# Who asks for the transfer of the negated maxima in a windowed attention and SwiGLU kernel

## The chip, the core and the metric

The kernel runs on one core of a Trainium2 chip. The metric is the device time of one execution in microseconds (us), lower is better. The kernel before was run three times; the table below has the times, and the profile is of one more execution.

## The reference

`x` is 2048 tokens of 512 values in fp32. With `xn` the layer norm of `x`, two branches are computed and combined:

```python
xn = _layernorm(x, axis=-1)
s = _A_ref(xn, A_wqkv, A_wo)              # attention
g = _silu(_B_ref(xn, gate, up, down))     # (silu(xn @ gate) * (xn @ up)) @ down
return x + s * g
```

The attention has 32 heads of 16 values. A query sees the 256 keys up to its own (`0 <= q - k < 256`), the scores are scaled by 1/4 and go through a softmax, the outputs of the heads go through `wo`. The hidden width of the SwiGLU branch is 1792.

## The kernel before, in words

**Tiling.** The tokens are cut into four chunks of 512 (`TC`), the heads into eight groups of four (`NG`). A unit `u` is one group in one chunk, `c, g = divmod(u, 8)`, so there are 32 units. The dense work (projections `a`, values `vp`, gate `g` and up `u`, down `d`, output `s`) is done in fp32 accuracy by splitting each operand in a high and a low part (`wh`, `wl`, `xh`, `xl`, `hh`) and adding three products; all of these matmuls stand in one helper at line 463. TensorE works in two halves of 64 rows, each with its own list of matmuls, and the two lists run beside each other.

**A unit of attention.** In the order in which it happens:

1. `load_qk` (line 917) loads queries and keys of the unit from DRAM into `qs[u % 3]` and `ks[u % 3]`. Queries and keys fill 48 of the 64 rows of each half, and a 49th row of the keys holds ones.
2. `max_pair` (line 946) multiplies queries by keys (`b`, line 960), and VectorE takes the masked maximum of each row into a column of `m` (line 968). There are 16 such maxima steps in a unit.
3. `max_turn` (line 988) transposes `m` with two matmuls on TensorE into the bank `mt` (line 994), the first and second half of the rows; between them stands a one-column copy on VectorE (`ho`, line 460).
4. `neg` (line 1007) runs on ScalarE and writes the negated maxima to `ms` in SBUF (line 1009).
5. `put` (line 1015) moves `ms`, 8 KB, into rows 48 and 112 of `qs[u % 3]`. So the 49th row of the queries, times the 49th row of ones in the keys, subtracts the maximum within the matmul.
6. `prob_pair` (line 1063) multiplies keys by queries with 49 rows (`c`, line 1111). ScalarE takes the exponential (`p`, line 1072), GpSimd masks it (lines 1085 and 1089).
7. `pv_visit` (line 1128) multiplies `p` by the values (`pv`, line 1148). ScalarE and VectorE add the two halves (`ev`, lines 1164 and 1169), and the result goes to DRAM, to be divided and used by `Wo`.

**What sets the order.** Nothing is reordered after the program is written. A planner in the program itself walks a virtual clock and writes out the instructions of all engines in the order of its own plan. It keeps a queue for VectorE (`V`), ScalarE (`S`), GpSimd (`G`) and for DMA issues (`D`, all on SyncE's queue); `do` (line 107) adds an operation with the time from which it can run, a cost, and a slack that sets its priority. When an operation is planned, what follows is told that it ends at the engine's free time plus a latency (`LAT`: 0.17 us for ScalarE, line 105). `dma` (line 115) is `do` for the queue `D`: an issue costs 0.5 us, must wait until the oldest of the last eight transfers (`lanes`) is planned to have landed, and its own landing is planned as

```python
stream_at[0] = max(stream_at[0], t) + kb / 230.0
done = stream_at[0] + LAND          # LAND = 3.5
```

The dense units have a fixed order, made ahead of time (`dense_order`, line 1217). Attention work comes in three streams with due times in units of dense progress (`plan_attention`, line 1195): the maxima from `u + 0.02`, the transposes at `u + 0.8`, the first `c` at `u + 1.07`, `pv` at `u + 1.89`. In the main loop (line 1386) a piece of attention work goes ahead of dense work when it is due and its inputs are planned to be ready. For `c` that is `prob_ready` (line 1055): the transfer of the maxima has landed by plan (`ms_at`), two banks are free, and there is room for `p`.

**Queues.** All transfers go through `move` (line 90), by default on SyncE's queue. Only two of the first four tiles of `x` are asked for by ScalarE, in its own queue. The engines wait for each other through semaphores in the order written.

Of the kernel before, what the change touches and what calls it, by code (L numbers as in the profile page):

```python
# [55 lines left out]
def tile_window_attention_swiglu_gate(  # L56
# [10 lines left out]
    nc = tc.nc  # L67
# [16 lines left out]
    def sb(name, shape, dtype, kind, n):  # L84
        return pers.tile(shape, dtype, name=name, tag=ring(kind, n), bufs=1)

    def f32(ap):
        return ap.bitcast(F32)

    def move(dst, src, eng=nc.sync):  # L90
        if dst.dtype == F32R:
            dst = f32(dst)
        if src.dtype == F32R:
            src = f32(src)
        eng.dma_start(dst, src)  # L95
# [11 lines left out]
    def do(e, ready, cost, fn, then=None, slack=0.5, can=None, lat=None):  # L107
        seq[0] += 1
        queue[e].append((ready + slack, seq[0], ready, cost, fn, then, can, LAT.get(e, 0.0) if lat is None else lat))
# [5 lines left out]
    def dma(ready, fn, then=None, slack=0.5, kb=256, can=None, e="D"):  # L115
        def begun_at(t):
            stream_at[0] = max(stream_at[0], t) + kb / 230.0
            done = stream_at[0] + LAND
            lanes.append(done)
            lanes.pop(0)  # L120
            if then:
                then(done)

        do(e, ready, 0.5, fn, begun_at, slack, lambda: lanes[0] <= now[0] and (can is None or can()), 0.0)
# [52 lines left out]
    def bank(pool, name):  # L177
        tag = min((v, k) for k, v in pool.items() if v is not None)[1]
        pool[tag] = None
        return ps.tile([P, 512], F32, name=name, tag=tag, bufs=1), tag  # L180
# [5 lines left out]
    qs = [pers.tile([P, 2, TC], F32R, name=f"q{i}") for i in range(3)]  # L186
# [181 lines left out]
    def half(r):  # L368
        return slice(R * r, R * r + R)
# [89 lines left out]
    def handover(pb):  # L459
        nc.vector.tensor_copy(pers.tile([MW, 1], F32, name="ho", tag=ring("ho", 2), bufs=1), pb[:MW, 0:1])  # L460
# [454 lines left out]
    ms_at = {}  # L915
# [72 lines left out]
    def max_turn(u, r):  # L988
        if r == 0:
            mtp[u] = [*bank(rb_free, f"mt{u}"), None]  # L990
        pb, tag, _ = mtp[u]

        def go():
            nc.tensor.matmul(
                pb[:MW, R * r : R * r + R], mts[u % 2][half(r), :], ident[half(r), half(r)],
                is_transpose=True, start=True, stop=True,
            )

        if r == 0:
            def after(t):  # L1000
                mtp[u][2] = t

            extra[0].append((128, go, lambda t: do("V", t, 0.09, lambda: handover(pb), after, -1.0)))
            return
        box = []

        def neg():
            box.append(sb(f"ms{u}", [16, P], F32R, "ms", 2))
            nc.scalar.activation(box[0], pb[:16, :P], AF.Copy, scale=-1.0)

        def after_neg(t):
            rb_free[tag] = t
            dma(t, put, lambda t: ms_at.__setitem__(u, t), -3.0, 8)

        def put():
            move(qs[u % 3][48 : 113 : 64], box[0])

        extra[1].append((128, go, lambda t: do("S", t, 0.25, neg, after_neg, -1.0)))

# [173 lines left out]
    def plan_attention():  # L1195
        for u in range(NU):
            c = u // NG
            if u:
                marks.append((u - 1 + 0.3, load_qk, (u,)))
            for n in range(8):  # L1200
                streams[0].append((u + 0.02 + 0.1 * n, max_ready, max_pair, (u, n // 4, n % 4)))
            streams[0].append((u + 0.8, turn_ready, max_turn, (u, 0)))
            streams[0].append((u + 0.8, turn_ready, max_turn, (u, 1)))
            ne = 3 if c == 0 else 4
            for n in range(2 * ne):
                streams[1].append((u + 1.07 + 0.1 * n, prob_ready, prob_pair, (u, n // 2, n % 2)))
            streams[1].append((u + 1.89, pv_ready, pv_visit, (u, tuple(range(ne)))))
        for c in range(1, NCH):
            marks.append((8 * c - 4.9, load_x, (c,)))
            for k in range(KC):  # L1210
                streams[2].append((8 * c - 3.3 + 0.25 * k, xt_ready, xt_turn, (c, k)))
        for s in streams:
            s.reverse()
        marks.sort(key=lambda m: -m[0])
# [73 lines left out]
    extra = [[], []]  # L1288
# [97 lines left out]
    while True:  # L1386
# [11 lines left out]
        if not any(extra):  # L1398
            s = work[0] / PACE - LEAD
            for st in sorted(streams, key=lambda st: st[-1][0] if st else 1e9):  # L1400
# [7 lines left out]
                t = need(*a)  # L1408
# [20 lines left out]
        if os.environ.get("VIRT"):  # L1429
            u, i = stream[min(pos[0], len(stream) - 1)]  # L1430
# [40 lines left out]
```

## Time and profile before

| | |
|---|---|
| runs of the kernel before | 871.76 us median of 3 (870.12 to 876.5) |
| profiled execution, its own time | 871.37 us |
| its span, first to last instruction | 869.7 us |
| mean granted clock of TensorE | 0.999 |
| bytes moved by DMA, mean rate | 139.62 MB, 161 GB/s |

Lines of the profile name an engine, a line of the kernel, and the tile written and read (`q<-ms` is the transfer of this case). PE is TensorE's matmul, PEld its weight load, DVE VectorE, ACT ScalarE, POOL GpSimd, SP SyncE. A `q` behind an engine's name (SPq, ACTq) means its sequencer, which issues transfers. Times in a timeline are the start from the span's beginning and the length, both in us; a bracket gives the idle time of the engine before it and what ended that. A wait for several semaphores is put down to the one that came last. In lists of waits the numbers are the total, how often, and the longest.

### The profile page before, as it was taken

How to read it: one execution, taken by the hardware profiler on the slowest of the kernel's cores; microseconds unless marked ns; L12 is line 12 of the kernel's file. 1: busy time of each engine (PE TensorE's matmuls, PEld its weight loads, DVE VectorE, ACT ScalarE, POOL GpSimd, SP SyncE). 2: the span in 40 equal slices, each digit the busy share in tenths (PEclk: the TensorE clock that was granted, in tenths of full speed). 3: DMA queues.
4: the chain of work that ended last, by engine and by line, in shares of the span. 5: the costliest groups of instructions: out<-in, count | busy, mean ns of one | idle time of the engine just before them, and what ended most of it. 6: DMA issues, size and time to landing. Idle time of an engine off the chain costs nothing.

```text
span 869.7 us, 30126 instructions
## 1 busy us (share of the span) xinstructions
PE 859.5 (99%) x11966; PEld 798.1 (92%) x11966; DVE 499.1 (57%) x1650; ACT 489.9 (56%) x1046; POOL 627.4 (72%) x871
## 2 busy tenths in 40 slices
PE   9999999999999999999999999999999999999997
PEld 8899889899889998999999999899999999999897
DVE  5364466654765565766576666566555765554234
ACT  3345565555666466655566556655656665666431
POOL 5556587667777778767696798676768688869771
PEclk9999999999999999999999999999999999999999
DMA  5765846567676984766677987546666779644352
GB/s 148 187 167 121 221 115 168 126 162 167 148 198 180 251 201 105 152 156 133 155 184 194 214 200 181 129 145 151 158 150 173 174 187 209 162 130 112 108 126 74
DMA packets 69488, 139.62 MB, mean 161 GB/s; under 512 B 14546, under 2 KB 23250, under 8 KB 69348
## 3 DMA queue, kind: packets, MB, share of 16 engines
q1 hardware_dynamic: 69060, 137.18, 64.1%
q8 instruction: 94, 1.54, 0.8%
q10 hardware_dynamic: 288, 0.52, 0.2%
q14 instruction: 46, 0.38, 0.2%
HBM read 107.74 MB, written 29.62 MB: 158 GB/s over the span
## 4 chain that ended last, share of the span: by engine, by line
PE 93%; DMA 3%; DVE 1%; SPq 1%; POOL 0%; issue 0%; ACT 0%; ACTq 0%; DVEq 0%; POOLq 0%
PE u L463 18%; PE d L463 18%; PE g L463 17%; PE a L463 11%; PE pv L1148 8%; PE s L463 6%; PE c L1111 5%; PE vp L463 5%; PE b L960 4%; DMA q<-ms 1%; DMA r<-rd 1%; DMA xt<-x 1%; SPq L95 1%; DVE xt L291 0%; PE xp L481 0%
## 5 line engine op out<-in xcount | busy, mean ns | idle before, releaser
L434 POOL TENSOR_TENSOR wl<-wr,wh 128x512 fp32r<-128x512 f32 (+3 forms) x258 | 306.8, 1208 | 89.4 <-ACT wh L431 86.9
L968 DVE CUSTOM_DVE_ANT_0 jk<-b,maskb 128x384 bf16<-128x384 f32 (+2 forms) x512 | 271.5, 530 | 130.1 <-PE b L960 64.5
L1072 ACT ACTIVATE p<-c 128x384 f32<-128x384 f32 (+1 forms) x480 | 208.8, 489 | 127.1 <-PE c L1111 106.5
L463 PE MATMUL d<-wh,hh 64*128 64x256 f32 x1792 | 258.2, 278 | 0.0
L463 PEld LDWEIGHTS d<-wh,hh 64*128 64x128 f32 x1792 | 222.9, 185 | 1.0 <-issue 0.6
L463 PE MATMUL d<-wl,hh 64*128 64x256 f32 x896 | 201.3, 277 | 0.0
L431 ACT ACTIVATE wh<-wr 128x512 fp32r<-128x512 f32 (+3 forms) x258 | 142.2, 593 | 51.2 <-PE d L463 11.1
L463 PE MATMUL u<-xh,wh 64*128 64x512 f32 x448 | 167.3, 396 | 0.0
L463 PE MATMUL g<-xh,wh 64*128 64x512 f32 x448 | 167.2, 396 | 0.0
L463 PE MATMUL u<-xl,wh 64*128 64x512 f32 x448 | 166.9, 396 | 0.0
L463 PE MATMUL u<-xh,wl 64*128 64x512 f32 x448 | 166.9, 396 | 0.0
L463 PE MATMUL g<-xl,wh 64*128 64x512 f32 x448 | 166.5, 395 | 0.0
L463 PE MATMUL g<-xh,wl 64*128 64x512 f32 x448 | 164.8, 394 | 0.0
L1085 POOL TENSOR_SCALAR_AFFINE_SELECT p<-p 128x256 f32<-128x256 f32 x256 | 103.7, 410 | 77.1 <-ACT p L1072 75.6
L463 PEld LDWEIGHTS d<-wl,hh 64*128 64x128 f32 x896 | 144.4, 185 | 0.3
L960 PE MATMUL b<-k,q 48*128 48x384 f32 (+1 forms) x512 | 119.2, 333 | 0.0
L1111 PE MATMUL c<-q,k 49*128 49x384 f32 (+1 forms) x704 | 115.5, 302 | 2.3 <-DMA q<-ms 1.2
L1089 POOL TENSOR_SCALAR_AFFINE_SELECT p<-p 128x256 f32<-128x256 f32 x224 | 91.6, 410 | 13.2 <-ACT p L1072 13.1
L463 PE MATMUL a<-xh,wh 64*128 64x512 f32 x256 | 97.2, 394 | 0.0
L463 PE MATMUL a<-xh,wl 64*128 64x512 f32 x256 | 96.4, 392 | 0.0
L616 POOL TENSOR_TENSOR hh<-h,hh 128x512 fp32r<-128x512 f32 x56 | 72.5, 1295 | 33.0 <-ACT hh L612 32.7
L463 PE MATMUL a<-xl,wh 64*128 64x512 f32 x256 | 96.2, 393 | 0.0
(109 smaller groups left out, 2096.6 us busy)
## 6 DMA issues: line engine op xcount, KB each, us to landing
wr<-wgu SPq DMA_DIRECT2D x112, 256.0 KB
k<-qkd SPq DMA_DIRECT2D x48, 192.0 KB
wr<-wqk SPq DMA_DIRECT2D x32, 256.0 KB
qkd<-qkh SPq DMA_DIRECT2D x32, 256.0 KB
qkd<-qkl SPq DMA_DIRECT2D x32, 256.0 KB
q<-qkd SPq DMA_DIRECT2D x64, 128.0 KB
wr<-wdn SPq DMA_DIRECT2D x32, 256.0 KB
od<-ev SPq DMA_DIRECT2D x32, 256.0 KB
```

Of the source, the lines that this page charges most:

```text
L95: eng.dma_start(dst, src)
L431: nc.scalar.activation(hi[0][pr, a:b], raw[pr, a:b], AF.Copy)
L434: nc.gpsimd.tensor_tensor(lo[0][pr, a:b], raw[pr, a:b], f32(hi[0][pr, a:b]), op=ALU.subtract)
L463: return nc.tensor.matmul(pb, a, b, start=first, stop=last, skip_group_check=True)
L616: nc.gpsimd.tensor_tensor(hl[:, 1, :], self.h, f32(hl[:, 0, :]), op=ALU.subtract)
L960: nc.tensor.matmul(pb[:, :w], qs[u % 3][r : r + 48, p, qb * P : (qb + 1) * P], ks[u % 3][r : r + 48, p, lo : lo + w], start=True, stop=True,)
L968: nc.vector.tensor_tensor_reduce(junk[:, :n], pb[:, :n], maskb[:, 3 * P - n :], 1.0, -3.0e38, ALU.add, ALU.max, m[:, col : col + 1],)
L1072: nc.scalar.activation(t[:, h, :], pc[:, a:b], AF.Exp, scale=DH ** -0.5)
L1085: nc.gpsimd.affine_select(s, s, [[0, 2], [1, P]], ALU.is_ge, 0.0, base=0, channel_multiplier=-1)
L1089: nc.gpsimd.affine_select(s, s, [[0, 2], [-1, P]], ALU.is_gt, 0.0, base=0, channel_multiplier=1)
L1111: nc.tensor.matmul(pc[:, at0 : at0 + w], ks[u % 3][r : r + 49, p, k0 : k0 + P], qs[u % 3][r : r + 49, p, qb * P : qb * P + w], start=(i == ...
L1148: nc.tensor.matmul(pbs[r][0][32 * j : 32 * j + 32, q0:q1], vt[half(r), (4 * c + kb) % VT, VW * (4 * g + j) : VW * (4 * g + j) + 32], t[hal ...
```

## The change

`put` is gone as an operation of its own. `neg` now asks for the transfer itself, on ScalarE's queue, right behind the negation. In the plan ScalarE is charged 0.6 us in place of 0.25 for the two together. The transfer no longer goes through the plan's DMA queue `D` with its lanes and its stream of bytes; it is taken as landed 3.4 us after the planned end of ScalarE's operation. The bank of `mt` is given back in the plan at that same planned end.

```diff
@@ -1007,15 +1007,13 @@
         def neg():
             box.append(sb(f"ms{u}", [16, P], F32R, "ms", 2))
             nc.scalar.activation(box[0], pb[:16, :P], AF.Copy, scale=-1.0)
+            move(qs[u % 3][48 : 113 : 64], box[0], nc.scalar)
 
         def after_neg(t):
             rb_free[tag] = t
-            dma(t, put, lambda t: ms_at.__setitem__(u, t), -3.0, 8)
-
-        def put():
-            move(qs[u % 3][48 : 113 : 64], box[0])
-
-        extra[1].append((128, go, lambda t: do("S", t, 0.25, neg, after_neg, -1.0)))
+            ms_at[u] = t + 3.4
+
+        extra[1].append((128, go, lambda t: do("S", t, 0.6, neg, after_neg, -1.0)))
```

## The prediction

> **What bounds the kernel now.** I read the page first, then a table of three stretches, then who TensorE waited for.
>
> ```profile
> span 869.7 us, 30126 instructions
> PE 859.5 (99%) x11966; PEld 798.1 (92%) x11966; DVE 499.1 (57%) x1650; ACT 489.9 (56%) x1046; POOL 627.4 (72%) x871
> PEclk9999999999999999999999999999999999999999
> ```
>
> ```profile
> 0.00:15.00 15.00, 13.08 (x88) 12.68 (x89) 8.78 (x27) 4.59 (x8) 8.82 (x19) 1.00 0.55 161
> 15.00:853.00 838.00, 834.60 (x11723) 773.71 (x11722) 483.16 (x1611) 484.69 (x1038) 618.56 (x852) 1.00 0.66 162
> 853.00:870.00 17.00, 11.87 (x159) 11.66 (x158) 7.16 (x14) 0.60 (x1) 0.00 (x0) 0.92 0.18 63
> ```
>
> The columns after the length of each stretch are TensorE, its weight loads, VectorE, ScalarE, GpSimd, then clock, DMA share and GB/s. Between the start and the last output, 15 to 853 us, TensorE shows 834.60 of 838.00 us busy, at a granted clock of 1.00. So 838.00 - 834.60 = 3.40 us is all the idle time that any edit can remove there in plain sight. The first 15 us and the last 17 us hold nothing that the edit touches. No count of matmuls changes. The list of TensorE's waits, longest first in total (us, times, longest), names most of it:
>
> ```profile
> PE c L1111 <- DMA q<-ms: 1.2, 2, 0.6
> PE c L1111 <- DVE m L968: 1.1, 1, 1.1
> PE mt L994 <- DVE ho L460: 0.9, 1, 0.9
> ```
>
> The moved transfer is the first row: two waits out of 32 units. In the chain that ended last it stands twice as well (start, length):
>
> ```profile
> 54.09 5.34 DMA q<-ms
> ...
> 242.00 6.08 DMA q<-ms
> ```
>
> Both run from the issue to the matmul that waited. The timelines of ScalarE, SyncE, VectorE and TensorE around the three waits of c (start, length):
>
> ```profile
> 53.80 0.27 ACT L1009 ACTIVATE ms<-mt 16x128 fp32r<-16x128 f32 x1
> 54.09 0.56 SPq L95 DMA_DIRECT2D q<-ms  x1
> 59.57 0.74 PE L1111 MATMUL c<-q,k 49*128 49x256 f32 x8 [0.61 <-DMA q<-ms]
> ...
> 96.23 0.27 ACT L1009 ACTIVATE ms<-mt 16x128 fp32r<-16x128 f32 x1 [0.68 <-PE vp L463]
> 97.96 0.60 SPq L95 DMA_DIRECT2D q<-ms  x1
> 104.28 0.08 DVE L968 DVE_READ_ACCUMULATOR2_ANT m<- 128x1 f32 x1
> 104.50 0.50 PE L1111 MATMUL c<-q,k 49*128 49x256 f32 x4 [1.10 <-DVE m L968]
> ...
> 238.49 0.27 ACT L1009 ACTIVATE ms<-mt 16x128 fp32r<-16x128 f32 x1 [1.13 <-PE mt L994]
> 240.12 1.80 SPq L95 DMA_DIRECT2D wr<-wqk  x2
> 242.00 0.60 SPq L95 DMA_DIRECT2D q<-ms  x1
> 248.22 0.50 PE L1111 MATMUL c<-q,k 49*128 49x256 f32 x4 [0.57 <-DMA q<-ms]
> ```
>
> Unit 0: the negation ends at 53.80 + 0.27 = 54.07, SyncE issues 0.02 us later, and the transfer itself is slow. Unit 8: the negation ends at 238.76, but SyncE is still issuing weight loads and comes to the transfer at 242.00, 3.24 us late. Unit 2: SyncE is 1.46 us late (97.96 - 96.50), yet the matmul starts 0.14 us after VectorE's last m ended (104.28 + 0.08 = 104.36), so this wait is for a bank that VectorE was still reading, and I do not count it as the transfer's.
>
> **What leaves SyncE.** In 32 units one issue and the wait ahead of it leave SyncE's queue. Its rows, from the view of the tile ms, with the two transfers that ScalarE asks for at the start beside them for the price there (min/median/max ns), and from SyncE's waits:
>
> ```profile
> L1009 ACT ACTIVATE ms<-mt x32: 247/266/268, 53.8 to 788.0; 16x128 fp32r<-16x128 f32 x32
> L95 SPq DMA_DIRECT2D q<-ms x32: 554/602/667, 54.1 to 788.3; - x32
> ```
>
> ```profile
> L95 SPq DMA_DIRECT2D xt<-x x2: 400/406/412, 0.8 to 1.2; - x2
> L95 ACTq DMA_DIRECT2D xt<-x x2: 404/434/463, 0.8 to 1.2; - x2
> ```
>
> ```profile
> SPq L95 <- ACT ms L1009: 19.7, 11, 4.7
> SPq L95 <- DMA r<-rd: 11.7, 7, 3.2
> SPq L95 <- DMA q<-qkd: 10.4, 20, 1.3
> ```
>
> SyncE is rid of 32 x 0.602 = 19.3 us of issuing and of 19.7 us in which it stood for a negation in 11 units. What was queued behind were weight loads, stores and the next queries. They can start up to 4.7 us sooner. TensorE's waits show no weight, so the worth is 0 on the path, and a sooner load meets the DMA engines at a mean share of 0.66. If that cover were gone the 19.7 us would be the most it could be worth.
>
> **What ScalarE gets.** One DMA issue per unit behind the negation. The trace has ScalarE's issues only for x: 434 ns against SyncE's 406 for the same thing, so I price the new one as SyncE's, 0.602, plus 0.02 to wait for the negation's write (unit 0 above). That is 32 x 0.62 = 19.9 us in which ScalarE's sequencer starts nothing else; with its 489.9 us of work it is taken for about 510 us, 59% of the span. The negation and its transfer together hold ScalarE for 0.27 + 0.62 = 0.89 us; the plan charges 0.6, so ScalarE will run 0.29 us behind the plan in each unit. Queued behind the issue are the weight splits (L431), the copies of pv, hidden units and the exponentials. Two examples of a following instruction that stands right there:
>
> ```profile
> 332.95 0.27 ACT L1009 ACTIVATE ms<-mt 16x128 fp32r<-16x128 f32 x1
> 333.13 0.84 ACT L431 ACTIVATE wh<-wr 128x256 fp32r<-128x256 f32 x2
> ...
> 123.44 0.25 ACT L1009 ACTIVATE ms<-mt 16x128 fp32r<-16x128 f32 x1
> 123.59 0.57 ACT L1164 ACTIVATE ev<-pv 128x512 f32<-128x512 f32 x1
> ```
>
> Today these start 0.18 and 0.15 us after the negation's start, while it still runs. With the issue between they start 0.89 us after it: 0.71 us later where ScalarE has no idle time, 32 x 0.71 = 22.7 us if it were so in every unit. What hides it is ScalarE's own idle time and the lead of the weights. ScalarE waits and GpSimd waits, then TensorE's weight loads:
>
> ```profile
> ACT p L1072 <- PE c L1111: 106.5, 105, 3.9
> POOL wl L434 <- ACT wh L431: 86.9, 47, 5.5
> ```
>
> ```profile
> PEld pv L1148 <- POOL wl L434: 0.6, 2, 0.4
> PEld b L960 <- ACT p L1072: 0.2, 1, 0.2
> ```
>
> ScalarE stands idle 106.5 us ahead of exponentials, 1.0 us per wait, and TensorE's side waits 0.8 us in all for what ScalarE and GpSimd make of weights and exponentials. I price the delay on TensorE at 0; the bounds are 0 and 22.7 us, and the first is far nearer to the 0.8 us.
>
> **What the plan does with it.** The order on every engine is written out by the planner, so its times move matmuls. Before, the maxima counted as landed no sooner than 0.25 + 0.17 + 8/230 + 3.5 = 3.95 us after the negation's start, and later when the planned DMA queue or its eight lanes were full. Now it is always 0.6 + 0.17 + 3.4 = 4.17 us. In free units the first c may be placed 0.22 us later, in crowded ones some us sooner. But c has a due time too (u + 1.07 against u + 0.8 for the transposes). Two later units show where that puts c now:
>
> ```profile
> 339.69 0.40 PE L1111 MATMUL c<-q,k 49*128 49x256 f32 x4
> ...
> 439.67 0.53 PE L1111 MATMUL c<-q,k 49*128 49x256 f32 x6
> ```
>
> The first comes 339.69 - 333.22 = 6.5 us after its negation and has nothing to gain. c of unit 8 comes 248.22 - 238.76 = 9.5 us after it; without the 3.24 us of SyncE it need not wait. Unit 0's c comes 5.5 us after, and its slow transfer goes into a queue with no load ahead of it. Other reordering I cannot work out; I take 0, with -3.4 (all visible idle time gone) and +3.4 (as much added) as bounds.
>
> **The sum.** The profiled execution took 871.37 us, 869.7 of span and 1.7 around it; the median of the runs is 871.76, 0.04% above, so no correction. Minus 0.61 (unit 0), minus 0.57 (unit 8), 0 for unit 2, 0 for SyncE, 0 for ScalarE: 871.37 - 1.18 = 870.2 us. If unit 2's 1.10 is the transfer's as well, 869.1.
>
> The Trainium skill speaks against unit 0's part: "DMA: Bandwidth & Descriptors", section "Issuing engines are not separate DMA queues", says that transfers asked for by different engines run on the same 16 DMA engines and interleave, and that a second issuing engine saves only the issue time. By that rule the 5.34 us of unit 0 stay and its 0.61 with them. The same page's "Queues, rings and completion order" says that each DMA engine takes turns between queues by packets, by which the small transfer would pass the loads. No transfer in this trace's steady part runs in ScalarE's queue, so the trace cannot decide.
>
> **The rivals.**
>
> *The transfer is as slow in its new queue.* What is late in unit 0 is not SyncE: it issued 0.02 us after the negation, and 5.34 us followed. If that is the DMA engines' load (0.66 mean share) and not the place in SyncE's queue, only unit 8's 0.57 goes, 870.8; and where c moves up to the flat 4.17 us while the transfer takes 5 to 6 us, new waits of about 1 us come in a few crowded units, so 871 to 873; I take 871.8. For it: unit 0's rows. Against: a c at its due time, 6.5 us behind as in the row at 339.69, comes after such a landing.
>
> *ScalarE is held, slower than before.* Place: the new issue on ScalarE. SyncE's rows with DMA names show that an issue can stand until an earlier transfer has landed (the planner's eight lanes, which no longer count this one): up to 3.2 us each. On SyncE this cost nothing. On ScalarE everything behind it stands: weight splits, copies, exponentials. The two rows give (11.7 + 10.4) / 27 = 0.82 us per wait. In the 21 units where SyncE did not stand for the negation its queue was busy; 21 x 0.82 = 17.2 us and the 22.7 of the issues are 39.9 us, 1.25 per unit, against 1.0 us of idle time ahead of an exponential. It decides from there: 0.25 x 32 = 8 us come through, 870.2 + 8 = 878.2 us. In another mixture, seven holds of 3.2 us, 2.2 each over the cover, add 15.4: 885.6. Against: TensorE waits 0.8 us today for all that ScalarE feeds.
>
> *The new order is luckier.* All of the 3.40 us goes: 868.0. For it: of TensorE's waits 1.1 and 0.9 us fall to c and mt, the two matmuls on either side of the transfer, whose places the plan now chooses anew. Against: what ends these two is VectorE's m and ho, and neither is touched.
>
> *It does not do what it says*: ScalarE's part of the plan orders another instruction between, and the transfer starts no sooner. The move stands in the same function as the negation, so I give this no chance of its own.
>
> **How the numbers follow.** Forecast 0.54, with its own range 868 to 872.5; as slow 0.24 (871.8); held 0.12 (878.2, up to 885.6); luckier 0.10 (868.0). The range: below 868 I leave room for idle time that the modelled ends of matmuls hide, to 866; above it reaches to the held case's middle, 878. About 1 in 10 is left out, nearly all above. One per cent is 8.7 us, about what a measurement can tell here (the three runs span 870.12 to 876.5). Faster by that needs 863, more than twice the visible idle time: 0.03. Slower needs 880.5, the upper part of the held case: 0.06. Same: 0.91.
>
> **What would show it.** Right: q<-ms under ScalarE's queue, 32 issues of about 0.6 us, each right behind its negation; the row of c waiting for q<-ms gone or under 0.3 us; SyncE's row for ms gone; ScalarE's busy time the same 490 us, with TensorE's 834.6 of 838 kept within 2 us. Wrong: ScalarE's sequencer standing for an earlier transfer by over 1 us in many units and weights or banks appearing in TensorE's waits (held), or c waiting for q<-ms in more units than two (as slow). A time under 866 or over 878 would mean that the new order itself moved far more than the transfer.

## The result, and the profile after

The changed kernel takes 903.66 us (median of 4 runs, 898.97 to 908.13) against 870.94 for the kernel before on the same chips: a ratio of 1.0356, 95% interval 1.0319 to 1.0393. It is slower by 3.6%, where 870.2 was forecast. The profiled execution took 905.47 us.

The page of the changed kernel, and its table of the stretch from 15 us to the last output (TensorE is the first number behind the length):

```profile
span 903.7 us, 29991 instructions
PE 872.3 (97%) x11966; PEld 805.3 (89%) x11966; DVE 498.9 (55%) x1650; ACT 493.1 (55%) x1046; POOL 629.0 (70%) x871
PEclk9999999999999899999889999999999989999999
```

```profile
15.00:887.00 872.00, 847.64 (x11722) 781.19 (x11721) 483.22 (x1611) 487.93 (x1038) 619.78 (x852) 0.98 0.64 156
```

The span grew by 903.7 - 869.7 = 34.0 us, all of it in this stretch (872 against 838). Of that, TensorE's idle time is 872.00 - 847.64 = 24.36 us in place of 3.40, so 21.0 us more, and its busy time 847.64 in place of 834.60, 13.0 us more for the same matmuls. The other engines' busy time hardly changed (ScalarE's most, 487.93 against 484.69). TensorE's waits and the chain that ended last say what the idle time is:

```profile
PE c L1109 <- DMA q<-ms: 23.6, 7, 7.2
```

```profile
54.10 5.20 DMA q<-ms
96.83 6.37 DMA q<-ms
240.05 6.39 DMA q<-ms
292.17 6.13 DMA q<-ms
443.40 7.17 DMA q<-ms
524.29 7.46 DMA q<-ms
720.65 10.05 DMA q<-ms
```

The wait for the moved transfer, 1.2 us in two units before, is 23.6 us in seven units now. The other waits beside c that stood in the list before are gone (1.1 and 0.9 us), which is why the idle time grew by somewhat less than 22.4. Unit 0 can be held beside its rows of before: 5.20 us from issue to landing in place of 5.34. In a queue with nothing ahead of it the transfer took as long.

Most of the added busy time is the clock. Between 15 us and the last output the trace has four stretches with a granted clock of 0.50 (the number behind the engines); everywhere else there it is 1.00:

```profile
296.39:303.22 6.83, 4.79 (x44) 4.82 (x46) 1.37 (x6) 1.26 (x3) 2.00 (x4) 0.50 0.90 263
446.58:456.82 10.24, 6.12 (x45) 6.15 (x47) 1.82 (x6) 3.25 (x8) 5.84 (x9) 0.50 0.67 150
531.91:535.32 3.41, 3.41 (x25) 3.41 (x27) 0.57 (x2) 1.36 (x3) 1.93 (x3) 0.50 0.87 224
729.88:736.71 6.83, 5.87 (x32) 5.24 (x34) 1.28 (x5) 2.06 (x5) 2.04 (x4) 0.50 0.81 160
```

TensorE is busy in 4.79 + 6.12 + 3.41 + 5.87 = 20.19 of these 27.31 us; the rest of them lies inside the waits. Half the clock for 20.19 us is an estimate of 10.1 us lost. The other 2.9 of the 13.0 us came at full clock, and what made them is open (e1, below, shows 838.00 us of busy time in its own stretch, 3.4 more than the kernel before, at a clock of 1.00). So 34 us = 21 us of waiting, about 10 us of slow clock and about 3 us that no row explains.

Unit 16 shows the whole course (ScalarE, then TensorE; start, length):

```profile
436.83 0.27 ACT L1009 ACTIVATE ms<-mt 16x128 fp32r<-16x128 f32 x1
443.40 0.52 ACTq L95 DMA_DIRECT2D q<-ms  x1
444.01 0.60 ACT L1162 ACTIVATE ev<-pv 128x512 f32<-128x512 f32 x1 [6.92 <-DMA wr<-wdn]
```

```profile
443.10 0.39 PE L463 MATMUL g<-xh,wh 64*128 64x512 f32 x1
450.70 0.80 PE L1109 MATMUL c<-q,k 49*128 49x256 f32 x4 [7.21 <-DMA q<-ms]
451.30 0.62 PE L463 MATMUL g<-xl,wh 64*128 64x512 f32 x1
```

The negation ends at 437.10. ScalarE then stands 6.30 us before it asks for the transfer. The bracket on ev's row names what ev itself waited for, not what held the issue: that one takes a completion semaphore whose last user was SyncE's load r<-rd, issued at 432.35 and landed at 443.32, 0.08 us before the issue. TensorE comes to c at 450.70 - 7.21 = 443.49, 6.4 us behind the negation, but only 0.09 us after the issue, and waits out the whole landing. Afterwards a matmul of 512 columns takes 0.62 us in place of 0.39, at half the clock.

### The profile page after: what moved, and what is told of

Its sections match the earlier page's. It is cut to its first block, busy times and chain, and to the rows that moved or that the text cites. A ratio compares the mean times of both kernels' runs of the same rounds, so it can differ in the third digit from the quotient of the medians.

```text
span 903.7 us, 29991 instructions
## 1 busy us (share of the span) xinstructions
PE 872.3 (97%) x11966; PEld 805.3 (89%) x11966; DVE 498.9 (55%) x1650; ACT 493.1 (55%) x1046; POOL 629.0 (70%) x871
## 4 chain that ended last, share of the span: by engine, by line
PE 86%; DMA 11%; DVE 1%; issue 1%; SPq 1%; POOL 0%; ACT 0%; ACTq 0%; DVEq 0%
PE d L463 17%; PE u L463 17%; PE g L463 16%; PE a L463 10%; PE pv L1146 7%; PE c L1109 6%; DMA q<-ms 5%; PE vp L463 4%; PE b L960 4%; PE s L463 4%; DMA r<-rd 1%; DMA q<-qkd 1%; DMA wr<-wgu 1%; DMA xr<-x 1%; DMA xt<-x 1%
## 5 line engine op out<-in xcount | busy, mean ns | idle before, releaser
L463 PEld LDWEIGHTS d<-wl,hh 64*128 64x128 f32 x896 | 146.8, 185 | 0.1
L1109 PE MATMUL c<-q,k 49*128 49x384 f32 (+1 forms) x704 | 120.3, 309 | 23.6 <-DMA q<-ms 23.6
L1109 PEld LDWEIGHTS c<-q,k 49*128 49x128 f32 x704 | 90.1, 191 | 30.5 <-issue 23.8
L463 PE MATMUL a<-xl,wh 64*128 64x512 f32 x256 | 98.1, 398 | 0.0
```

The source lines that it names most:

```text
L463: return nc.tensor.matmul(pb, a, b, start=first, stop=last, skip_group_check=True)
L1109: nc.tensor.matmul(pc[:, at0 : at0 + w], ks[u % 3][r : r + 49, p, k0 : k0 + P], qs[u % 3][r : r + 49, p, qb * P : qb * P + w], start=(i == ...
```

## The experiments

Theory P: the plan is at fault. It takes the transfer as landed at a flat time, without the loads in front of it, and so places c ahead of a transfer that is still on its way. Theory Q: ScalarE's queue is at fault, by holding ScalarE or by carrying the transfer more slowly. The first three runs part these two, and e4 was to part two causes within P. Ratios are to the kernel before on the same chip.

**e1: ScalarE's queue, counted in the plan as before.**

```diff
+            stream_at[0] = max(stream_at[0], t) + 8 / 230.0
+            done = stream_at[0] + LAND
+            lanes.append(done)
+            lanes.pop(0)
-            ms_at[u] = t + 3.4
+            ms_at[u] = done
-        ... do("S", t, 0.6, neg, after_neg, -1.0)
+        ... do("S", t, 0.6, neg, after_neg, -1.0, lambda: lanes[0] <= now[0])
```

> The transfer stays in ScalarE's queue, but the plan counts it as it did before the change: it waits for one of the eight lanes, takes its share of the planned stream, and lands 3.5 us after that. Theory P (the plan's flat 3.4 us puts the first c ahead of a transfer that is still on its way; the queue itself costs nothing): TensorE's wait of c for q<-ms falls from 23.6 to under 4 us, the clock stays at 0.99 or more, and the time is 868 to 875 us. Theory Q (ScalarE's queue is the fault, by holding ScalarE or by a slower transfer): the waits and the time stay within a third of the way, above 890 us.

Measured: 875.44 us, ratio 1.0048 (1.0023 to 1.0073), clock 0.998. The waits and the clock are as P expected; the time is 0.44 us above its range, and the interval does not reach 1, so the queue is not free as P had it. TensorE's waits, and ScalarE in unit 16:

```profile
PE c L1113 <- DMA q<-ms: 2.5, 3, 1.3
```

```profile
429.22 0.27 ACT L1009 ACTIVATE ms<-mt 16x128 fp32r<-16x128 f32 x1
436.14 0.52 ACTq L95 DMA_DIRECT2D q<-ms  x1
436.76 0.60 ACT L1166 ACTIVATE ev<-pv 128x512 f32<-128x512 f32 x1 [7.27 <-DMA wr<-wdn]
```

ScalarE is held even longer than in the changed kernel, 6.65 us, and the transfer still takes 6.6 us to land; yet c comes 13.3 us behind the negation, because the plan counts the loads, and waits 0.61 us of these.

**e2: SyncE's queue, flat in the plan.** The kernel before, with one line changed:

```diff
-            dma(t, put, lambda t: ms_at.__setitem__(u, t), -3.0, 8)
+            dma(t, put, lambda d: ms_at.__setitem__(u, max(t + 3.75, now[0])), -3.0, 8)
```

> The other half alone: the transfer is asked for by SyncE as before the change, with its place in the plan's DMA queue, but the plan takes it as landed at the changed kernel's flat time, 4.17 us after the negation's start, as soon as it is issued. Theory P: c is placed too early again, at least as often as in the changed kernel because SyncE comes late as well; waits of c for q<-ms of 15 to 40 us and a time of 890 to 920 us. Theory Q: the queue is the old one, so 868 to 878 us.

Measured: 899.27 us, ratio 1.0334 (1.0268 to 1.04), clock 0.981. Without anything on ScalarE the loss is there:

```profile
PE c L1111 <- DMA q<-ms: 21.8, 8, 4.4
```

**e3: the changed kernel with 6.6 us.**

```diff
-            ms_at[u] = t + 3.4
+            ms_at[u] = t + 6.6
```

> The changed kernel with the flat landing time raised from 3.4 to 6.6 us, nothing else. Theory P: most landings of the changed kernel (1.7 to 7.5 us behind the issue, one of 10.0) fall inside it; only the units in which the issue itself was held, by 1.5 to 6.3 us, and the one slow landing remain, so waits of c of 5 to 12 us and 876 to 888 us. Theory Q: ScalarE's holds and the issues are unchanged, the time stays above 895 us.

Measured: 888.9 us, ratio 1.0173 (1.0117 to 1.023), clock 0.988. The wait is within what P expected, the time 0.9 us above its range, and each of the three waits that stayed has a stretch of half clock in it or behind it:

```profile
PE c L1109 <- DMA q<-ms: 8.1, 3, 3.2
```

**e4: the changed kernel with the lanes counted, the landing flat.** As e1, but `ms_at[u] = t + 3.4`.

> The changed kernel with the lanes alone counted: the negation waits in the plan until a lane is free, and the transfer takes a lane, but its landing stays flat at 3.4 us. Of theory P this parts the held issue from the slow landing. If the held issues of ScalarE (1.5 to 6.3 us in four units) are what made the waits long, their units' waits go (2.8 + 4.3 + 7.2 + 3.2 of the 23.6 us) and the time is near 880 us; if the slow landing is most of it, the time stays above 890 us.

Measured: 897.55 us, ratio 1.0293 (1.0247 to 1.034), above the 890 us that stood for the slow landing. But the run does not take the holds away: counting the lanes in the plan does not keep ScalarE from being held (1.77, 4.02, 7.35 and 2.63 us in units 8, 10, 16 and 19), so the time alone does not part the two. The waits fall by less than half:

```profile
PE c L1112 <- DMA q<-ms: 13.2, 6, 4.5
```

All of that fall is in the four held units, whose waits go from 17.5 to 6.6 us (none is left in unit 16); in units 0, 2 and 27, where nothing was held, they go from 6.2 to 6.6. In the changed kernel the holds of these four units were 1.99, 4.49, 6.30 and 1.49 us. An estimate from these rows: with the smaller of hold and wait taken off in each unit, 14.0 of the 23.6 us would not be there. So both a held issue and a slow landing are missing from the flat 3.4 us.

What e1 has beyond e4 is the planned stream of bytes in the landing time, and with it the waits go from 13.2 to 2.5 us. This term leaves room for both: in unit 16 of e1 TensorE comes to c 12.65 us behind the negation, where hold and landing take 6.65 and 6.57.

**e5: the changed kernel with 10.5 us.** As e3, with `t + 10.5`.

> The changed kernel with the flat landing raised to 10.5 us. If the early placing of c is all that matters, one unit is left (its issue was held 6 us and its transfer took 5 to 7), so waits of c for q<-ms of 0 to 3 us, no half clock before the last output, and 872 to 880 us; the attention of each unit comes some 3 us later than due, which the dense work covers. If c placed late costs as much as c placed early, the time is above 885 us.

Measured: 881.09 us, ratio 1.0094 (1.0064 to 1.0125). No wait of c for q<-ms is left in TensorE's list, as expected, and the time is 1.1 us above the expected range, because the clock was halved once, which was not expected:

```profile
276.00:286.00 10.00, 10.00 (x66) 10.00 (x66) 2.45 (x11) 1.75 (x5) 1.81 (x5) 0.50 0.78 231
```

That is 5 of the 8 us by which it is above the kernel before (873.01 on this chip). In the 14 us before, TensorE shows only 0.56 us of idle time; what lowered the clock there is not settled. A flat time gets rid of the waits only where it is long enough for the worst unit, and then it is still 0.9% above the kernel before.

**e6: the kernel before with 1.5 us more in the plan.** `ms_at.__setitem__(u, t + 1.5)` in place of `t`.

> The kernel before, on SyncE's queue and counted in the plan as there, with the planned landing 1.5 us later. If the two or three waits of c in the kernel before (1.2 to 2.3 us) are a gain to be had by the plan alone, they go and the time is 868 to 870.5 us, 0.1 to 0.3% less; if the new order gives as much back, it is within 0.3% either way.

Measured: 873.62 us, ratio 1.001 (0.9989 to 1.0032). No gain. The waits moved to other units (2.7 us in two), and the longer one has a stretch of half clock behind it:

```profile
PE c L1111 <- DMA q<-ms: 2.7, 2, 2.4
```

**e7: GpSimd's queue, counted plan.** As e1, with `nc.gpsimd` for `nc.scalar` in the move.

> The counted plan of e1 with the transfer asked for by GpSimd in its queue in place of ScalarE's. It shows whether a transfer from a third queue passes the loads. If the load on the DMA engines makes the landing late, it lands as late in busy units (5 to 7 us behind the negation in units 0, 2 and 8) and later in quiet ones; if the queues of SyncE and ScalarE share something that GpSimd's does not, it lands within 3 us everywhere. GpSimd stands for each negation, so the time should be 875 to 900 us.

Measured in a single run: 878.9 us, beside a median of 873.01 for the kernel before, clock 0.999. The view of the tile ms gives the landing for this queue:

```profile
L95 POOL DMA_DIRECT2D q<-ms x32: 575/580/728, 55.3 to 794.9; - x32
...
DMA to landing us min/median/max: 1.7/3.8/7.4
```

From 1.7 to 7.4 us behind the issue: a third queue does not pass the loads either.

**e8: more load on SyncE's queue, counted plan.** As e1, with three transfers of 256 KB ahead of each negation:

```diff
+            for n in range(3):
+                move(extra_load[u, n], x[n * P : n * P + P, :])
             nc.scalar.activation(box[0], pb[:16, :P], AF.Copy, scale=-1.0)
```

> The counted plan of e1 with three transfers of 256 KB from DRAM to DRAM asked for on SyncE's queue ahead of each negation, work that nobody reads and the plan does not count. Nothing is added to ScalarE's queue. If load on the DMA engines makes the landing late whatever the queue, the units whose transfer landed 1.7 us behind its issue (1, 3, 5, 12, 13, 15, 30) now land 4 to 8 us behind it, and c waits for q<-ms 30 to 120 us in all with the clock halved many times, 920 to 1050 us. If ScalarE's queue passes SyncE's loads, those landings stay below 2.5 us and the waits below 20 us.

Measured in a single run: 892.82 us, clock 0.990. Neither expectation held. By the last completion count of each transfer in the trace, the seven quiet units landed 1.71, 2.05, 1.69, 2.94, 2.90, 2.23 and 2.20 us behind their issue, later than 1.7 in five of them but nowhere near 4. The added transfers were there: the trace has them issued 1.0 to 4.7 us ahead of the moved one in these units, and 20 of the 21 had not landed when it was issued. So two or three of them on their way did not make a late landing. The waits are below 20 us:

```profile
PE c L1116 <- DMA q<-ms: 12.8, 9, 3.3
```

The run shows that load costs time even with the counted plan when the plan does not know of it, and leaves open how much of a landing each load makes.

**e10: the changed kernel's plan, SyncE's queue.** The purest exchange: the queue takes no part in the plan, so the written orders of TensorE, VectorE and GpSimd are the same.

```diff
-            move(qs[u % 3][48 : 113 : 64], box[0], nc.scalar)
+            move(qs[u % 3][48 : 113 : 64], box[0])
```

> The changed kernel's own plan, instruction for instruction on TensorE, VectorE and GpSimd, with one thing set back: the transfer is asked for by SyncE, at the same place in the program. If the plan's flat 3.4 us is the whole loss, the queue makes no difference: waits of c for q<-ms of 18 to 30 us and 893 to 912 us. If ScalarE's holds (4.5 and 6.3 us in units 10 and 16) made the long waits, the time falls to 875 to 888 us.

Measured: 897.86 us, ratio 1.0289 (1.0255 to 1.0324), clock 0.985.

```profile
PE c L1109 <- DMA q<-ms: 16.2, 5, 5.1
```

The wait is 2 us under the expected range, the time inside it. The expectation took the holds to go with ScalarE's queue. They do not: SyncE too stood 3.42, 2.85 and 5.12 us behind the negations of units 8, 10 and 16. In unit 16 the transfer of r<-rd that used the same completion semaphore before landed at 441.41, 0.06 us ahead of this issue:

```profile
436.09 0.27 ACT L1009 ACTIVATE ms<-mt 16x128 fp32r<-16x128 f32 x1
441.47 0.56 SPq L95 DMA_DIRECT2D q<-ms  x1
448.09 0.80 PE L1109 MATMUL c<-q,k 49*128 49x256 f32 x4 [5.06 <-DMA q<-ms]
```

So it shows what the exchange of the queue is worth, not what the holds are.

**e9: e1's plan, SyncE's queue.** The same one-line exchange in e1.

> The same exchange in e1: its counted plan kept, the transfer asked for by SyncE at the same place. It tells what of e1's 0.5% over the kernel before is ScalarE's queue and what the new order. If the hold of ScalarE is the price, it comes back to 870 to 872 us and the ratio's interval reaches 1.000; if the order is, it stays at 874 to 877 us.

Measured: 871.77 us, ratio 0.998 (0.9956 to 1.0003), clock 0.998. So what e1 lost is the price of ScalarE's queue, not of the new order. No wait of c for q<-ms is left in its list. It has the lowest ratio of all versions, but its interval reaches no difference from the kernel before.

The four runs make a table of ratios:

| plan of the landing | SyncE asks | ScalarE asks |
|---|---|---|
| counted in lanes and stream | e9: 0.998 (0.9956 to 1.0003) | e1: 1.0048 (1.0023 to 1.0073) |
| flat 3.4 us | e10: 1.0289 (1.0255 to 1.0324) | the change: 1.0356 (1.0319 to 1.0393) |

The flat time costs 1.0289 / 0.998 = 1.031 in one column and 1.0356 / 1.0048 = 1.031 in the other, 27 us. ScalarE's queue costs 1.0068 and 1.0065, 6 us; the intervals of the upper row do not touch, those of the lower overlap by 0.0005. Within a row the two ran on different chips; by the times alone the queue costs 3.7 and 5.8 us. The lists of waits say where: c waits for q<-ms 23.6 us in the changed kernel against 16.2 in e10, and 2.5 in e1 against none in e9. So most of the queue's price is again the transfer that comes late.

## Why the prediction was wrong, step by step

**What bounds the kernel: right.** TensorE was the bound, and the 3.40 us of idle time was the most that could be gained in sight. The wait of unit 2 is not as clear as the step has it: the trace has the transfer landing at 104.36, the moment at which VectorE's m ended, so these rows do not tell which of the two c waited for. What was not said is that a bound engine with a fixed order has no floor on the other side: any wait put into its queue is paid in full.

**What leaves SyncE: right, worth 0.** SyncE's wait for ms falls from 19.7 us in 11 places to 1.2 in 2, and nothing on TensorE got faster by it.

**What ScalarE gets: the price of 0 was too low.** The issue itself took 520 ns against the 602 that were taken:

```profile
L95 ACTq DMA_DIRECT2D q<-ms x32: 505/520/1134, 54.1 to 821.8; - x32
```

But the queue costs 6 us (e1 against e9, the change against e10). The rival of the held ScalarE named the place and priced it at 8 us; the longest hold, 6.30 us in unit 16, is twice its 3.2, and the 21 units in which it took SyncE's queue to be busy were 14 by the trace (issue over 0.2 us behind the negation). Its path was another: it expected what stands behind the issue on ScalarE (weights, copies, exponentials) to come late, and the list of TensorE's matmul waits in the changed kernel has none for ScalarE; in e1 it has one, of 0.6 us. What the hold delayed was the transfer itself. The 0.8 us that the step held against it was also read short: GpSimd's masked exponentials stand in the same list of weight loads of the kernel before, which makes 1.9:

```profile
PEld pv L1148 <- POOL p L1089: 1.1, 3, 0.4
```

The trace says why ScalarE can be held by loads that SyncE asked for: all 745 transfers take the same eight completion semaphores in turn, in program order, whichever engine asks, and in unit 16 the last user landed 443.32 - 437.10 = 6.22 us after the negation's end. That this reuse is what holds ScalarE rests on the times and the order in the traces; no run gave the transfers other semaphores.

**What the plan does with it: this step failed.** It says that in crowded units the first c "may be placed ... some us sooner", that unit 8's c "need not wait", and that unit 0's "slow transfer goes into a queue with no load ahead of it", and takes the rest of the reordering as 0, with +3.4 us as the bound. Put right: in crowded units c was placed sooner and the transfer was not sooner. In unit 8 TensorE came to c 5.7 us behind the negation in place of 8.9, and its wait grew from 0.57 to 2.79 us. The cause lay in the two formulas that the step itself compares. The old one holds the stream of planned bytes and the lanes; in the crowded units these terms, not SyncE's queue, were what placed c late, and they were right to. The step read them as a delay that the change takes away, where they were a forecast of what is still on its way. That holds the issue, and a late landing goes with it. e2 shows this without ScalarE (899.27 us), e1 shows the reverse (875.44 us with ScalarE's queue): the flat time costs 27 us.

**The bound of 3.4 us had no ground.** It took the idle time in sight as the measure of what a new order can add. The rows gave a better one: the transfer took 5.34 and 6.08 us in the two units shown, the plan was to allow 3.4 from then on in every unit, and each difference stands in front of the engine that sets the time.

**The rival that came nearest was mis-sized.** "The transfer is as slow in its new queue" is what happened, with a chance of 0.24. It gave "about 1 us in a few crowded units". Measured: seven waits of 0.4 to 7.2 us, 23.6 in all, and about 10 us of slow clock that no part of the prediction held.

**The two rules.** The Trainium skill's "DMA: Bandwidth & Descriptors", section "Issuing engines are not separate DMA queues", spoke against the gain of unit 0, and the traces agree with it: 5.20 us in ScalarE's queue against 5.34 in SyncE's, and up to 7.4 in GpSimd's. The other rule that was weighed, in that page of the Trainium skill under "Queues, rings and completion order", is that each DMA engine takes turns between queues by packets. The prediction read it as a small transfer that passes the loads; the landings of 5.20 and 6.37 us with nothing ahead in ScalarE's queue (units 0 and 2) do not show that.

**The slow clock.** In the changed kernel the clock stood at half for 3.4 to 10.2 us in or just behind the waits of 4.25, 7.21, 3.23 and 4.78 us, and not behind that of 2.79 us. The length of the wait alone does not decide it: in e3 all three waits (1.80, 3.10 and 3.19 us) had half clock behind them, in e6 one of 2.4 us had, and in e4 one of 3.43 us had not. Two stretches came behind shorter pauses: at 216.54 in e2 (0.33, 0.71 and 0.45 us in the 5 us before) and at 447.15 in e4 (1.30 and 0.94). The Trainium skill's "TensorE: Matmul & The Clock Gate", section "Part 1: The HAM clock gate", says that TensorE falls to half its clock after an idle window of about 3.4 us that runs freely. The traces agree in that longer waits bring it and that the length does not settle it alone; the half clock behind 1.80 and 2.4 us is less idle time than a whole such window, and what else counted there is open.

## What to carry to other kernels

Where a kernel's order comes from a plan, an edit that moves an operation out of the plan's accounts is two edits, and the accounts can matter more than the queue: here 27 us against 6. Before moving a small transfer to an idle engine's queue, ask what made it late: where it was the other transfers on their way, another queue did not make it sooner here, and the engine that asks may be held for a landing it has nothing to do with. On an engine that is 99% busy, price the wait of a matmul that is placed too early at its full length, and add the slow clock, which came behind most waits from about 2 us on, not behind each, and a few times behind less.

## What the runs showed of the hardware that was not expected

In these traces the landing of an 8 KB transfer within SBUF goes with the load and not with the queue. The same table for six landings of the changed kernel, from the issue to about the first packet (units 0, 1, 2 and 3) and to the landing (units 20 and 28); the last two numbers are DMA share and GB/s:

```profile
54.10:58.20 4.10, 4.10 (x44) 3.96 (x40) 2.39 (x11) 1.10 (x3) 0.62 (x2) 1.00 0.74 247
74.70:75.80 1.10, 1.10 (x36) 0.58 (x40) 0.61 (x1) 0.00 (x0) 0.30 (x1) 1.00 0.00 0
96.80:101.70 4.90, 4.90 (x115) 4.04 (x113) 0.78 (x2) 1.43 (x4) 0.00 (x0) 1.00 0.70 228
123.60:124.80 1.20, 1.20 (x14) 1.20 (x12) 0.38 (x2) 0.48 (x1) 1.09 (x1) 1.00 0.00 0
552.70:557.78 5.08, 5.08 (x95) 4.18 (x99) 2.90 (x9) 2.50 (x6) 1.30 (x1) 1.00 0.89 225
751.00:754.72 3.72, 3.72 (x112) 2.70 (x110) 0.38 (x2) 2.27 (x4) 2.38 (x2) 1.00 0.87 207
```

With the DMA engines empty it landed 1.72 and 1.75 us behind its issue (units 1 and 3), at a share of 0.74 and 0.70 it took 5.20 and 6.37. The share alone does not settle it: at 0.89 and 0.87 it took 5.08 and 3.72 (units 20 and 28). Nearer comes the number of other transfers that had been issued and had not landed, counted in the changed kernel's trace at the moment of the issue: with none to two of them the landing took 1.7 to 3.6 us, with five to seven 5.1 to 10.1. No run varied that number alone. Most of the time is not the moving: in units 0 and 2 the first packet began 4.15 and 4.93 us after the issue, against 1.17 and 1.16 in units 1 and 3, with nothing ahead of it in ScalarE's queue, and the last ended within 0.7 us of that. What holds the first packet so long while the DMA engines are a quarter idle is left open; nothing here tells the making of its descriptors from the wait for the engines it uses.
